# A spatial weight tile of a gated MLP scaled in quarters, three of them in earlier groups, with its row scales made in two parts

## The chip, the cores and the metric

The kernel runs on one core of a Trainium2 chip. The time is that of the device for one execution, in microseconds (us), and the median of several runs is given. The engines of the core are named as in the profile: PE (TensorE, matrix products), DVE (VectorE), ACT (ScalarE), POOL (GpSimd) and SP (SyncE, which here only issues transfers). Each engine works through its own list of instructions in order, and waits where an instruction needs what another engine or a transfer has not yet delivered.

## What is computed

The reference is a transformer block: attention in a dilated sliding window, then a gated MLP with a spatial weight. The change lies in the second half, of which this is the core (S = 2048 positions, D = 1024, F = 3584, Fh = 1792, bfloat16):

```python
def _B_ref(x, w_in, w_sp, b_sp, w_out):
    z = _gelu(jnp.einsum('bsd,df->bsf', x, w_in))
    z1 = z[..., :Fh].copy()
    z2 = _layernorm(z[..., Fh:], axis=-1)
    g = jnp.einsum('ts,bsf->btf', w_sp, z2) + b_sp[None, :, None]
    return jnp.einsum('bsf,fd->bsd', z1 * g, w_out)
h = x + _A_ref(_layernorm(x, axis=-1), A_wqkv, A_wo)
h2 = h + _B_ref(_layernorm(h, axis=-1), B_w_in, B_w_sp, B_b_sp, B_w_out)
```

`w_sp` is 2048 x 2048: a product over positions, not over features.

## The kernel before

The last part of the kernel, from line 1449 on, computes `g`, `z1 * g` and the product with `w_out`. It works in two halves (`pr` = 0 and 1), each for 1024 output positions. A half has seven **groups** (`i`, numbered through as `n` = 0 to 13), each of 256 features, and then four **tile pairs** (`q`, numbered through as `w` = 0 to 7), each of 256 positions times `w_out`.

Both products are done with seven block products in place of eight (Strassen's way with Winograd's sums). So PE's operands are partly blocks and partly sums of blocks, which DVE makes beforehand: `z_form` (line 1209) for a group, `s_form` (line 1447) for a tile pair, `t_forms` (lines 1185 to 1191) for the spatial weight of a half, and `wform` (line 1430) for `w_out`. A block product in a group is eight matmuls on PE (line 1274, in `times`); the results come out of PSUM by ACT copies (lines 1484, 1489, 1338), DVE additions (lines 1542, 1558, 1570, 1578) and POOL additions (lines 1505, 1545, 1546, 1565). In a tile pair POOL adds `p5` to `p7` (line 1660) and `u` to `p7` (line 1688), and DVE ends with a multiply-add of `p7` into the residual row `h2` (line 1709); then the rows are stored.

**The spatial weight** comes as four tiles `raw[0]` to `raw[3]` of 512 output positions each, 128 partitions x 16 x 512, transposed by the load (`load_raw`, line 1173). Tiles 0 and 1 belong to the first half, 2 and 3 to the second; `rawa` is the name of tiles 0 and 2 in the profile, `rawb` that of 1 and 3. In fp16 its products would leave the range of the type, so every row of `w_sp` is scaled by a power of two (`scale_raw`, line 1178, half a tile at a time, 128 x 4096, in place, bfloat16 to fp16) and the result is scaled back at the end (`rv`). How the scales come about: ACT sums the absolute values of each 128 rows (`row_sum`, line 1128), DVE makes the powers of two (`row_scales`, seven small instructions, lines 1132 to 1138), PE turns them from a column to a row (line 1498), ACT copies the row out of PSUM and stores it to DRAM (lines 1500, 1501), and SP loads it, spread over all partitions, into `rows` (`rows_in`, line 1158).

For the second half, the sums of the eight row blocks 8 to 15 are made in groups 1 to 4, two blocks in each. The scales of all eight are made in group 5, after the third product of the group, together with the level of `w_out` (`wout_level`, lines 1393 to 1398, which line 1499 turns on PE). Tile 2 comes in four loads of 128 positions in groups 2 to 5, and is scaled by halves: the first at the end of group 6, the second in tile pair 1. Tile 3 is loaded in tile pair 0 and scaled in tile pair 2, by halves as well, one ahead of and one behind line 1709. The sums of tiles 2 and 3 (`t_forms(1, ...)`) follow in tile pair 3, and PE's first products of group 7 are mixed in there.

Orders: the program's text gives the order on PE, DVE, ACT, POOL and, from the start of this part, SP (`manual_schedule`). Buffers are shared by rotation: two for `p7`, five for the forms, six banks of PSUM. The scheduler of the first part (class `Order`) is touched only in that two helpers take other arguments, with the same instructions as before.

Of the kernel before, what the change touches and what calls it, by code (L numbers as in the profile page):

```python
# [12 lines left out]
FP16 = mybir.dt.float16  # L13
I32 = mybir.dt.int32
ALU = mybir.AluOpType
# [7 lines left out]
P = 128  # L23
NT = S // P
CH = 512
NCH = S // CH
TPC = CH // P
TPP = 2 * TPC
# [18 lines left out]
HK = S // P // 2  # L47
# [21 lines left out]
class Order:  # L69
# [6 lines left out]
    def add(self, eng, us, fn, deps=(), prio=5.0, lat=0.1, take=None, free=None, table=None):  # L76
        o = _Op()
        o.eng, o.us, o.fn, o.prio, o.lat, o.free, o.table = eng, us, fn, prio, lat, free, table
        o.take = (take,) if isinstance(take, str) else take or ()
        o.deps = [d if isinstance(d, tuple) else (d, d.lat) for d in deps if d is not None]  # L80
        o.start, o.end, o.n = None, None, len(self.ops)
        self.ops.append(o)
        return o
# [49 lines left out]
def kernel(  # L133
# [13 lines left out]
    V, A, T = nc.vector, nc.scalar, nc.tensor  # L147
    dma = nc.sync.dma_start
# [14 lines left out]
    rs_d = dpool.tile([NT, P], BF16, name="rs_d")  # L163
# [3 lines left out]
    ident = cpool.tile([P, P], BF16, name="ident")  # L167
# [12 lines left out]
    rsc16 = cpool.tile([P, NT], BF16, name="rsc16")  # L180
    rscT = cpool.tile([P, P], BF16, name="rscT")
# [220 lines left out]
    add = o_.add  # L402
    G = {}
# [694 lines left out]
    raw, frm, wt_ = {}, {}, {}  # L1098
    wabs_ops = []
# [27 lines left out]
        h_ = wn[i][:, hf * D:(hf + 1) * D]  # L1127
        A.activation(h_, h_, ACTF.Abs, accum_out=wabs[:, i, hf:hf + 1])

    def row_scales(pr):  # L1130
        n = slice(pr * TPP, (pr + 1) * TPP)
        V.tensor_tensor(wlim[:, n], wabs[:, n, 0], wabs[:, n, 1], op=ALU.add)
        V.tensor_tensor(wlim[:, n], wlim[:, n], babs[:, n], op=ALU.add)
        V.tensor_scalar(wlim[:, n], wlim[:, n], 2.0 ** -40, 2.0 ** 60, op0=ALU.max, op1=ALU.min)
        V.tensor_scalar(wexp[:, n], wlim[:, n].bitcast(I32), 0x7F800000, None, op0=ALU.bitwise_and)
        V.tensor_scalar(rsc[:, n], wexp[:, n], -1.0, float(261 << 23), op0=ALU.mult, op1=ALU.add)
        V.tensor_scalar(rinv[:, n], wexp[:, n], float(-(7 << 23)), None, op0=ALU.add)
        V.tensor_copy(rsc16[:, n], rsc[:, n].bitcast(FP32))
# [13 lines left out]
        A.copy(rscT[0:TPP, :], wt_["ps"][0:TPP, 0, 0:P])  # L1152
        dma(rs_d[0:TPP, :], rscT[0:TPP, :])

    def rows_in(pr):
        if pr == 0:
            wt_["rows"] = zpools["z"].tile([P, S], BF16, name="rows")
        dma(wt_["rows"][:, 2 * pr * CH:(2 * pr + 2) * CH],
            rs_d[pr * TPP:(pr + 1) * TPP, :].rearrange("i p -> (i p)").unsqueeze(0).to_broadcast([P, 2 * CH]))

    def bias_in(pr):
        cols = slice(2 * pr * CH, (2 * pr + 2) * CH)
        wt_["b", pr] = wt_["rows"][:, 0:2 * CH] if pr else bp.tile([P, 2 * CH], BF16, name="brow", tag="xr", bufs=XRB)[:]
        dma(wt_["b", pr], B_b_sp[cols].unsqueeze(0).to_broadcast([P, 2 * CH]))

    def bias_rows(pr):
        cols = slice(2 * pr * CH, (2 * pr + 2) * CH)
        V.tensor_tensor(wt_["rows"][:, cols], wt_["rows"][:, cols], wt_["b", pr], op=ALU.mult)
# [6 lines left out]
    def scale_raw(c, k0, n=HK):  # L1175
        ks = slice(k0, k0 + n)
        rows = wt_["rows"][:, c * CH:(c + 1) * CH].unsqueeze(1).to_broadcast([P, n, CH])
        V.tensor_tensor(raw[c][:, ks, :].bitcast(FP16), raw[c][:, ks, :], rows, op=ALU.mult)  # L1178

    def t_forms(pr, n):  # L1180
        a, b = raw[2 * pr][:].bitcast(FP16), raw[2 * pr + 1][:].bitcast(FP16)
        if n < 3:
            frm[pr, n] = zpools["z"].tile([P, HK, CH], FP16, name=f"form{n}")
        if n == 0:
            V.tensor_tensor(frm[pr, 0][:], b[:, 0:HK, :], a[:, 0:HK, :], op=ALU.subtract)
        elif n == 1:
            V.tensor_tensor(frm[pr, 1][:], b[:, HK:NT, :], frm[pr, 0][:], op=ALU.subtract)
        elif n == 2:
            V.tensor_tensor(frm[pr, 2][:], a[:, HK:NT, :], frm[pr, 1][:], op=ALU.subtract)  # L1189
        else:  # L1190
            V.tensor_tensor(b[:, 0:HK, :], b[:, HK:NT, :], b[:, 0:HK, :], op=ALU.subtract)
# [46 lines left out]
    bs_ = add("ACT", 0.3, bias_size, [bt_], prio=2.0, free="acc")  # L1238
    level1 = w1_level()
# [17 lines left out]
        zpools["ps"] = ctx.enter_context(tc.tile_pool(name="psA", bufs=2, space=PSUM, side="right"))  # L1257

    def rows_first():
        rows_in(0)  # L1260
        bias_in(0)

    head(NCH - 1)
    rs_ = add("DVE", 1.0, lambda: row_scales(0), [G["avdone", NCH - 1], bs_, level1] + wabs_ops, prio=2.8)
    rt_ = add("PE", 0.1, rows_turned, [rs_], prio=0.5, take="acc", lat=0.2)
    ro_ = add("ACT", 0.3, rows_out, [rt_], prio=1.0, free="acc")
    rl_ = dma_op(4.0, rows_first, [(ro_, 2.5), G["close"]])
# [4 lines left out]
    def times(dst, wts, mov, first, lo=0, hi=HK, last=HK):  # L1272
        for k in range(lo, hi):
            T.matmul(dst, wts(k), mov(k), start=(first and k == 0), stop=(k == last - 1), skip_group_check=not first)  # L1274

    def slab(t):
        return lambda k: t[:, k, :]
# [45 lines left out]
    def bank(dt=FP32):  # L1323
        return psB.tile([P, CH if dt == FP32 else 2 * CH], dt, name="bank", tag="bank", bufs=6)
# [35 lines left out]
    kb = p2.tile([P, 8], BF16, name="kb", tag="kb", bufs=1)  # L1360
# [30 lines left out]
    def wout_level():  # L1391
        l2 = l1n.rearrange("p (f j) -> p f j", j=2)
        V.tensor_tensor(kf, l2[:, :, 0], l2[:, :, 1], op=ALU.max)
        V.tensor_tensor(kf, kf, rf, op=ALU.mult)
        V.tensor_reduce(kk[:, 0:1], kf, axis=AX.X, op=ALU.max)
        V.tensor_scalar(kk[:, 0:1], kk[:, 0:1], 2.0 ** -60, 2.0 ** 90, op0=ALU.max, op1=ALU.min)
        V.tensor_scalar(kk[:, 0:1].bitcast(I32), kk[:, 0:1].bitcast(I32), 0x7F800000, None, op0=ALU.bitwise_and)
        V.tensor_copy(kb[:, 0:1], kk[:, 0:1])
# [50 lines left out]
    for pr in range(NCH // 2):  # L1449
# [5 lines left out]
        for i in range(NQ):  # L1455
            n = pr * NQ + i
# [34 lines left out]
                seven()  # L1491
                times(k3[:], slab(zs[n, 4]), slab(b22), False)
            times(k2[:], slab(zs[n, 2]), slab(t2_), True)
            if pr == 0 and i == 5:
                row_scales(1)
                wout_level()
                turned = bank(BF16)
                T.transpose(turned[0:TPP, 0:P], rsc16[:, TPP:NT], ident[:])
                T.transpose(turned[0:1, P:2 * P], kb[:, 0:1], ident[:])
                A.copy(rscT[0:TPP, :], turned[0:TPP, 0:P])  # L1500
                A.dma_start(rs_d[TPP:NT, :], rscT[0:TPP, :])
            if n not in (0, 1, NQ, NQ + 1):
                row_two(n, b21)
            times(k4[:], slab(a22), slab(t4_), False)
# [14 lines left out]
            if more:  # L1519
                if n in (0, NQ):  # L1520
                    if n == 0:
                        z_form(n + 1, 3)
                    z_form(n + 1, 1)
                if n == NQ:
                    bias_rows(1)
                if n == 0:
                    V.memset(ones[:], 1.0)
                    feature_scales()
            elif pr == 1:
                for m in (3, 1, 2, 4):  # L1530
                    s_form(TPC, m, 0, NQ - 1)
            else:
                for fp in range(4, NQ):
                    wout_scaled(fp)
                scale_raw(2, 0)
            if n + 2 < 2 * NQ:
                load_z2f(n + 2, 1)
            if n == 5:
                rows_in(1)
            if n == 0:  # L1540
                z1_scaled(n)
            V.tensor_tensor(u[:], k2[:], p1[:], op=ALU.add)
# [48 lines left out]
        for q in range(TPC):  # L1591
# [109 lines left out]
                nc.gpsimd.tensor_tensor(p7[:], p7[:], u[:], op=ALU.add)  # L1701
            if pr:
                V.scalar_tensor_tensor(h1[:, 0:CH], k1[:], r1, h1[:, 0:CH], op0=ALU.mult, op1=ALU.add)
            if pr == 0 and q < 3:
                (lambda: None, lambda: scale_raw(2, HK), lambda: scale_raw(3, 0))[q]()
            if pr:
                V.scalar_tensor_tensor(h2[:, 0:CH], k4[:], r2, (u if end else p5)[:], op0=ALU.mult, op1=ALU.add)
            if not end:
                V.scalar_tensor_tensor(h2[:, CH:D], p7[:], r2, h2[:, CH:D], op0=ALU.mult, op1=ALU.add)  # L1709
            if end:  # L1710
                dma(out2d[t1_ * P:(t1_ + 1) * P, 0:CH], h1[:, 0:CH])
                dma(out2d[t2_ * P:(t2_ + 1) * P, :], h2[:])
                for n, (lo, hi) in enumerate(((0, cut), (cut, CH))):
                    V.scalar_tensor_tensor(h1[:, CH + lo:CH + hi], k3[:, lo:hi], r1, p1[:, lo:hi], op0=ALU.mult, op1=ALU.add)
                    (dma if n else A.dma_start)(out2d[t1_ * P:(t1_ + 1) * P, CH + lo:CH + hi], h1[:, CH + lo:CH + hi])
            else:
                if pr:
                    V.scalar_tensor_tensor(h1[:, CH:D], k3[:], r1, p1[:], op0=ALU.mult, op1=ALU.add)
                for t, hr in ((t2_, h2), (t1_, h1)):
                    dma(out2d[t * P:(t + 1) * P, :], hr[:])  # L1720
# [34 lines left out]
```

## Time and profile before

| | |
|---|---|
| median of 3 runs | 689.41 us (689.26 to 689.83) |
| the profiled execution | 689.43 us, span 687.6 us |
| PE busy | 679.7 us, 99% |
| DVE busy | 591.8 us, 86% |
| ACT, POOL busy | 357.5 us, 168.3 us |
| granted TensorE clock | 1.00 |

The span runs from the first to the last instruction. Group 0 begins at about 433 us, and a group takes some 12 us; the tile pairs of the first half lie from 512 to 554, group 7 starts in the course of pair 3, and the last pair ends at 684. A row of a timeline gives the start, the length, the engine, the line, the operation, the tiles (out<-in), the shape, and in brackets the idle time of the engine ahead of it with what ended it. Matmuls overlap: eight matmuls in a row take 1.9 us from start to end, but the next eight start 1.73 us after them.

### The profile page before, as it was taken

The numbers are of one execution on the slowest core, as the hardware profiler recorded it, in microseconds if no ns is written. First come the engines' busy times: TensorE is split into PE (matmuls) and PEld (weight loads), VectorE is DVE, ScalarE is ACT, GpSimd is POOL, SyncE is SP. The second block draws the span as 40 slices with busy tenths as digits, with TensorE's granted clock in tenths as the row PEclk, the third lists the DMA queues.
The fourth block names the chain that finished last, engine by engine and source line by source line (L and its number), as shares of the span: only waits on it lengthen the run. The fifth ranks groups of instructions, "written<-read, shape, count | busy, mean of one in ns | idle before, by whom it ended". The sixth has DMA issues, their size and how long they took to land.

```text
span 687.6 us, 9194 instructions
## 1 busy us (share of the span) xinstructions
PE 679.7 (99%) x3423; PEld 360.1 (52%) x3440; DVE 591.8 (86%) x750; ACT 357.5 (52%) x529; POOL 168.3 (24%) x147
## 2 busy tenths in 40 slices
PE   9999999999999999999999999999999999999997
PEld 6766666566645445444544467444444443444443
DVE  6899899998999989998897878997889999755565
ACT  4547652354229998774882556387671131324121
POOL 0100010010210101000120134474541316553442
PEclk9999999999999999999999999999999999999999
DMA  9979588667995469444483996999967214642031
GB/s 314 335 245 247 172 194 273 154 164 270 217 346 222 98 247 231 168 173 107 122 226 120 206 269 200 302 291 325 244 209 184 98 59 124 186 121 94 1 113 71
DMA packets 143933, 133.07 MB, mean 194 GB/s; under 512 B 68752, under 2 KB 115504, under 8 KB 143760
## 3 DMA queue, kind: packets, MB, share of 16 engines
q1 hardware_dynamic: 132720, 88.93, 45.3%
q0 software_dynamic: 8416, 34.80, 18.2%
q10 hardware_dynamic: 2752, 8.75, 3.8%
q8 instruction: 27, 0.44, 0.3%
q14 instruction: 18, 0.15, 0.1%
HBM read 75.25 MB, written 33.10 MB: 158 GB/s over the span
## 4 chain that ended last, share of the span: by engine, by line
PE 92%; DVE 7%; issue 1%; POOL 0%; DVEq 0%; ACT 0%
PE acc L468 22%; PE bank L1274 22%; PE acc L800 14%; PE acc L868 11%; PE banka L1274 8%; PE acc L723 8%; PE acc L1040 2%; PE acc L310 2%; DVE zs L1209 1%; PE wps L232 1%; DVE rawb L1178 1%; DVE hr L1709 1%; DVE bank L1692 1%; PE acc L1004 1%; DVE hr L1693 0%
## 5 line engine op out<-in xcount | busy, mean ns | idle before, releaser
L800 PE MATMUL acc<-win,hnT 128*128 128x512 bf16 (+1 forms) x501 | 97.4, 352 | 0.6
L800 PEld LDWEIGHTS <-hnT 128*128 128x128 bf16 x512 | 49.9, 98 | 47.5 <-issue 0.7
L532 DVE TENSOR_TENSOR prod<-qT,kT 128x4096 bf16<-128x4096 bf16 x32 | 72.7, 2283 | 1.6 <-ACT kT L474 1.3
L868 PE MATMUL acc<-hnT,win 128*128 128x512 bf16 x336 | 73.7, 379 | 0.0
L1274 PEld LDWEIGHTS <-zs 128*128 128x128 f16 x448 | 43.3, 98 | 54.9 <-DVE zs L1209 3.7
L479 ACT CAST stg<-acc 128x1024 bf16<-128x1024 f32 x36 | 36.4, 1012 | 61.2 <-PE acc L468 54.7
L468 PE MATMUL acc<-xnT,wk 128*128 128x512 bf16 x256 | 56.5, 379 | 0.0
L468 PE MATMUL acc<-xnT,wv 128*128 128x512 bf16 x256 | 56.4, 380 | 0.0
L723 PE MATMUL acc<-wo_sb,av_oT 128*128 128x512 bf16 x250 | 55.8, 379 | 0.3
L1274 PEld LDWEIGHTS <-z 128*128 128x128 bf16 x336 | 32.7, 98 | 40.3 <-DVE form L1189 1.2
L868 PEld LDWEIGHTS <-win 128*128 128x128 bf16 x336 | 32.7, 98 | 39.5 <-issue 0.7
L1274 PE MATMUL bank<-rawb,zs 128*128 128x512 f16 x224 | 52.8, 379 | 0.4 <-DVE zs L1209 0.4
L1274 PE MATMUL banka<-rawa,z 128*128 128x512 f16 x224 | 52.0, 379 | 0.0
L1274 PE MATMUL bank<-form,zs 128*128 128x512 f16 x224 | 50.9, 379 | 0.8 <-DVE zs L1209 0.8
L468 PEld LDWEIGHTS <-wk 128*128 128x128 bf16 x256 | 36.5, 143 | 19.0 <-issue 0.8
L468 PEld LDWEIGHTS <-wv 128*128 128x128 bf16 x256 | 36.5, 144 | 18.6 <-issue 0.5
L468 PE MATMUL acc<-xnT,wq 128*128 128x512 bf16 x192 | 41.9, 379 | 0.0
L723 PEld LDWEIGHTS <-av_oT 128*128 128x128 bf16 x256 | 24.9, 98 | 29.8
L807 ACT ACTIVATE u<-acc 128x1024 bf16<-128x1024 f32 (+1 forms) x32 | 29.2, 911 | 19.9 <-PE acc L800 19.7
L536 DVE TENSOR_TENSOR prod<-prod 128x2048 bf16<-128x2048 bf16 x32 | 38.7, 1216 | 0.0
L1274 PEld LDWEIGHTS <-sf 128*128 128x128 f16 x231 | 22.4, 98 | 26.3
L468 PEld LDWEIGHTS <-wq 128*128 128x128 bf16 x192 | 27.5, 143 | 13.9
(325 smaller groups left out, 1237.5 us busy)
## 6 DMA issues: line engine op xcount, KB each, us to landing
z<-z_d SPq DMA_DIRECT2D x28, 512.0 KB, 5.3
qkv_d<-stg SPq DMA_DIRECT2D x36, 256.0 KB, 4.6
wn<-in_B_w_sp_dram ACTq DMA_DIRECT2D x16, 512.0 KB, 4.8
z1c<-z_d SPq DMA_DIRECT2D x14, 512.0 KB, 4.8
z_d<-z1s SPq DMA_DIRECT2D x21, 256.0 KB, 2.6
z_d<-u SPq DMA_DIRECT2D x12, 448.0 KB, 2.6
av_y<-av_z POOLq DMA_DIRECT2D x4, 1024.0 KB, 9.8
av_oT<-av_zz POOLq DMA_DIRECT2D x4, 1024.0 KB, 15.1
```

What stands on the lines that cost most here:

```text
L232: T.matmul(wps[:], warm[:, 0:P], warm[:], start=True, stop=True)
L310: T.matmul(dst.rearrange("p (a b) -> p a b", b=P), wqs[:, kt, dl, :], xnT[0][:, lo:hi, kt, :], start=start, stop=stop)
L468: T.matmul(G[key][:, j, :].rearrange("p (a b) -> p a b", a=TPC), wv[:, kt, dl, :], xnT[c][:, :, kt, :], start=(kt == 0), stop=(kt == KT - 1))
L479: A.copy(stg[:], G[key][:])
L532: V.tensor_tensor(st["prod"][:], qT[:], kT[:, :, o:o + CH], op=ALU.mult)
L536: V.tensor_tensor(dst, p_[:, 0:4, :], p_[:, 4:8, :], op=ALU.add)
L723: T.matmul(st["acc", il][:, nh, :], oTs[c][:, dl, il * P:(il + 1) * P], wo_sb[:, dl, nh * CH:(nh + 1) * CH], start=(dl == 0), stop=(dl == ...
L800: T.matmul(accf[:, n0:n1], hnTs[c][:, il, kt, :], wins[hf][:, kt, n0:n1], start=(kt == 0), stop=(kt == KT - 1))
L807: A.activation(st["u", il][:, hf * 1024:hf * 1024 + wd], G["accz", c, il, hf][:].rearrange("p a b -> p (a b)")[:, 0:wd], ACTF.Gelu_apprx_t ...
L868: T.matmul(G["accy", c, fp][:, j, :].rearrange("p (a b) -> p a b", a=TPC), wt[:, kt, f0 * P:(f0 + 1) * P], hnTs[c][:, :, kt, :], start=(kt ...
L1040: T.matmul(d_, wt, mv, start=(not again and j == 0 and kt == 0), stop=(j == len(fps) - 1 and kt == 3), skip_group_check=bool(again))
L1274: T.matmul(dst, wts(k), mov(k), start=(first and k == 0), stop=(k == last - 1), skip_group_check=not first)
```

## The change

- `row_scales` and `rows_in` take a range of row blocks. The scales of blocks 8 to 11 are made, turned, stored and loaded in group 3, those of 12 to 15 in group 5. So the seven DVE instructions, the transposition on PE, ACT's copy and store and SP's load are there twice, each for four blocks.
- A new helper `scale_tile` scales a quarter of a tile: 128 of its 512 positions, through all 16 blocks (128 x 16 x 128). Tile 2 is scaled by it: quarters 0 and 1 in group 4, quarter 2 in group 5 ahead of the row scales, quarter 3 at the end of group 6 where its first half was scaled.
- The scaling of tile 2's second half in tile pair 1 is gone.
- In tile pair 2, line 1709 comes ahead of the scaling of tile 3's first half.

```diff
-    def row_scales(pr):
-        n = slice(pr * TPP, (pr + 1) * TPP)
+    def row_scales(lo, hi):
+        n = slice(lo, hi)
...
-        dma(wt_["rows"][:, 2 * pr * CH:(2 * pr + 2) * CH],
-            rs_d[pr * TPP:(pr + 1) * TPP, :].rearrange("i p -> (i p)").unsqueeze(0).to_broadcast([P, 2 * CH]))
+        dma(wt_["rows"][:, lo * P:hi * P],
+            rs_d[lo:hi, :].rearrange("i p -> (i p)").unsqueeze(0).to_broadcast([P, (hi - lo) * P]))
...
+    def scale_tile(c, il):
+        cols = slice(il * P, (il + 1) * P)
+        rows = wt_["rows"][:, c * CH + il * P:c * CH + (il + 1) * P].unsqueeze(1).to_broadcast([P, NT, P])
+        V.tensor_tensor(raw[c][:, :, cols].bitcast(FP16), raw[c][:, :, cols], rows, op=ALU.mult)
...
             times(k2[:], slab(zs[n, 2]), slab(t2_), True)
-            if pr == 0 and i == 5:
-                row_scales(1)
-                wout_level()
+            if pr == 0 and i == 4:
+                scale_tile(2, 0)
+                scale_tile(2, 1)
+            if pr == 0 and i in (3, 5):
+                t0 = TPP if i == 3 else TPP + TPC
+                if i == 5:
+                    scale_tile(2, 2)
+                row_scales(t0, t0 + TPC)
+                if i == 5:
+                    wout_level()
                 turned = bank(BF16)
-                T.transpose(turned[0:TPP, 0:P], rsc16[:, TPP:NT], ident[:])
-                T.transpose(turned[0:1, P:2 * P], kb[:, 0:1], ident[:])
-                A.copy(rscT[0:TPP, :], turned[0:TPP, 0:P])
-                A.dma_start(rs_d[TPP:NT, :], rscT[0:TPP, :])
+                T.transpose(turned[0:TPC, 0:P], rsc16[:, t0:t0 + TPC], ident[:])
+                if i == 5:
+                    T.transpose(turned[0:1, P:2 * P], kb[:, 0:1], ident[:])
+                A.copy(rscT[0:TPC, :], turned[0:TPC, 0:P])
+                A.dma_start(rs_d[t0:t0 + TPC, :], rscT[0:TPC, :])
...
-                scale_raw(2, 0)
+                scale_tile(2, 3)
...
-            if n == 5:
-                rows_in(1)
+            if n in (3, 5):
+                rows_in(TPP if n == 3 else TPP + TPC, TPP + TPC if n == 3 else NT)
...
-            if pr == 0 and q < 3:
-                (lambda: None, lambda: scale_raw(2, HK), lambda: scale_raw(3, 0))[q]()
             if pr:
                 V.scalar_tensor_tensor(h2[:, 0:CH], k4[:], r2, (u if end else p5)[:], op0=ALU.mult, op1=ALU.add)
             if not end:
                 V.scalar_tensor_tensor(h2[:, CH:D], p7[:], r2, h2[:, CH:D], op0=ALU.mult, op1=ALU.add)
+            if pr == 0 and q == 2:
+                scale_raw(3, 0)
```

More of the change, by code (lines that the diff above doesn't have):

```diff
@@ L1153, in rows_out, with rows_in @@
         dma(rs_d[0:TPP, :], rscT[0:TPP, :])
-    def rows_in(pr):
-        if pr == 0:
+    def rows_in(lo, hi):
+        if lo == 0:
             wt_["rows"] = zpools["z"].tile([P, S], BF16, name="rows")
-        dma(wt_["rows"][:, 2 * pr * CH:(2 * pr + 2) * CH],
-            rs_d[pr * TPP:(pr + 1) * TPP, :].rearrange("i p -> (i p)").unsqueeze(0).to_broadcast([P, 2 * CH]))
+        dma(wt_["rows"][:, lo * P:hi * P],
+            rs_d[lo:hi, :].rearrange("i p -> (i p)").unsqueeze(0).to_broadcast([P, (hi - lo) * P]))
     def bias_in(pr):
@@ L1259, in rows_first @@
     def rows_first():
-        rows_in(0)
+        rows_in(0, TPP)
         bias_in(0)
     head(NCH - 1)
-    rs_ = add("DVE", 1.0, lambda: row_scales(0), [G["avdone", NCH - 1], bs_, level1] + wabs_ops, prio=2.8)
+    rs_ = add("DVE", 1.0, lambda: row_scales(0, TPP), [G["avdone", NCH - 1], bs_, level1] + wabs_ops, prio=2.8)
     rt_ = add("PE", 0.1, rows_turned, [rs_], prio=0.5, take="acc", lat=0.2)
```

## The prediction

> **What bounds the kernel now.** I read the busy table first, then the chain of work that ended last, then the timelines of the engines in the last 250 us.
>
> ```profile
> PE 679.7 (99%) x3423; PEld 360.1 (52%) x3440; DVE 591.8 (86%) x750; ACT 357.5 (52%) x529; POOL 168.3 (24%) x147
> PE 92%; DVE 7%; issue 1%; POOL 0%; DVEq 0%; ACT 0%
> ```
>
> PE is busy 99% of the span, so an edit that moves vector work can only win what PE idles, and can lose as much as it makes PE wait. The chain names the one place where DVE sets the end (start, length, engine, tile, line):
>
> ```profile
> 538.37 2.20 DVE rawa L1178
> 540.57 1.67 DVE hr L1709
> ...
> 548.73 2.28 DVE rawb L1178
> 551.01 1.67 DVE hr L1709
> 552.68 2.20 DVE rawb L1178
> ```
>
> It runs on DVE from 533.15 to 582.65 without a break. The third spatial tile's second half (538.37) is in it, and so is the multiply-add of line 1709, 1.67 long here. PE in the same place (start, length, what, idle time before and its releaser):
>
> ```profile
> 567.06 1.90 PE L1274 MATMUL bank<-form,z 128*128 128x512 f16 x8 [0.71 <-DVE form L1189]
> ...
> 570.84 1.90 PE L1274 MATMUL bank<-rawb,zs 128*128 128x512 f16 x8 [0.16 <-DVE zs L1209]
> 573.50 3.70 PE L1274 MATMUL bank<-form,zs 128*128 128x512 f16 x16 [0.76 <-DVE zs L1209]
> ```
>
> A fourth wait, 0.27, stands at 582.65. What they cost in all: a block of eight matmuls takes 1.727 us (group 8 to 9, 584.38 to 596.47, is 12.09 for seven). From 554.10, the first block of the second half, to 641.36 there are 49 blocks, 84.62 us; they took 87.26. **PE loses 2.64 us there, and that is the most that the change can win.**
>
> **What is taken from that place.** The second half's scaling leaves: 2.28 by its row, 2.20 from its start to the next instruction. It would seem that line 1709 shrinks too, since it takes 0.74 at 530.18 and 1.75 behind each scaling, which would make 2.20 + 2 x 1.01 = 4.2 us. POOL's rows speak against that:
>
> ```profile
> 505.75 2.65 POOL L1505 TENSOR_TENSOR p<-p,p 128x512 f32<-128x512 f32 x1 [6.24 <-ACT p L1489]
> 548.97 3.16 POOL L1660 TENSOR_TENSOR p<-p,p 128x512 f32<-128x512 f32 x1 [2.19 <-ACT p L1651]
> ```
>
> The same additions take 1.26 to 1.27 alone. The one at 548.97 begins while DVE scales (548.73 to 551.01) and ends at 552.13, some 1.15 after that scaling; line 1709 begins at 550.92 and ends 0.54 after POOL. So the two take turns, and the 1.01 is POOL's turn, which will fall on another DVE instruction. The Trainium skill (SBUF — State Buffer, "Who interferes with whom") has this as a rule: a DVE instruction with two SBUF inputs and a GpSimd instruction that reads SBUF share a port, and the later one blocks wholly. By the rule the gain is the 2.1 below; by the plain subtraction it would be 4.2, cut to 2.64 by PE's idle time; this trace agrees with the rule.
>
> With turns the chain is, walked by the starts in the rows: line 1709 of pair 1 at 538.29 (POOL idle, 0.67 to the next start), forms of pair 3 at 538.96 and 539.50; POOL's addition, ready at 539.91, takes its 1.2 at 540.05; the other two forms 541.25 to 542.40 (the PE product that frees the last one's buffer ends at 540.7, so it isn't late). Line 1680 then starts at 542.40 where it was 544.69. The six instructions to line 1709 keep their spacing: 1709 of pair 2 at 546.44, now first; tile 3's first half 547.11 to 549.31; POOL (ready 548.9) 1.2; second half 550.50 to 552.70; line 1665; the first form tile at 553.38 instead of 555.47. **DVE arrives 2.09 earlier, and the swap by itself wins nothing**: it moves POOL's turn from line 1709 to the second scaling. Later instructions wait on DVE or on POOL behind it and shift alike, so PE keeps 2.64 - 2.09 = 0.55 of its loss. Bounds: 2.64 if POOL's turns fall into gaps, and 2.09 - 1.2 = 0.9 if one more falls on the chain.
>
> **What is added earlier.** Four quarters of 128x2048. No row has this shape with runs of 128; a quarter tile as 128x2048 in runs of 512 takes 1.21 to 1.22 (line 1178 in the first half, 1.14 from start to start), and the forms of line 1209 read runs of 128 at 0.68 for 1024, the same rate. I take 1.14; the upper bound is the 2.28 of a whole half.
>
> Two quarters come in group 4, ahead of line 1542:
>
> ```profile
> 478.96 0.68 DVE L1584 TENSOR_TENSOR zg<-zg,z1c 128x1024 f16<-128x1024 f16 x1
> 482.19 0.69 DVE L1542 TENSOR_TENSOR u<-bank,p 128x512 f32<-128x512 f32 x1 [2.55 <-PE bank L1274]
> ...
> 483.85 0.69 DVE L1558 TENSOR_TENSOR zg<-banka,rows 128x512 f16<-128x512 f32 x1 [0.37 <-PE banka L1274]
> ...
> 485.64 0.69 DVE L1570 TENSOR_TENSOR zg<-bank,p 128x512 f16<-128x512 f32 x1 [0.51 <-PE bank L1274]
> ```
>
> DVE waits 2.55 there for PE, and 2.28 fits. POOL's addition, ready at 481.0, waits to 481.9 and holds the next form to 483.1; the gaps of 0.37 and 0.51 take that up. Cost 0, with 3.43 - 2.28 = 1.15 to spare.
>
> Group 3 gets row scales for four tiles: seven small DVE instructions, 1.17 (490.97 to 492.14 in group 5), in DVE's 1.58 idle ahead of line 1542 (468.52 to 470.10); the sums they need were finished by ACT at 461.8. The result is there at 469.7, PE reaches its new transposition at 469.83. In group 5 the two transpositions take PE from 494.00 to 494.31, so one costs 0.1 to 0.3: **0.16**. ACT copies the result (0.25) and issues its store (0.53); waiting for PE it starts the row sums behind that some 2.1 later. Its gaps until line 1489 in group 4 are 0.66, 1.20 and 1.09, together 2.95: hidden; without them POOL's addition and the end of group 4 would come 2.1 later. The loads of the last two weight rows, issued by ACT, move from 473.08 to 475.2, and at 4.9 to landing arrive before their sums at 480.87.
>
> The row of scales must be in SBUF by 479.6. The store goes out at 470.4 to 470.9. The small store of group 5 was issued at 494.69 and read from 498.43, so it took at most 3.7; 256 KB stores land in a median of 2.0. The load stands on SP behind the one at 473.48, so it leaves at 473.9 to 474.2 and, at the 4.0 to 4.5 of its sisters (twice its size), lands by 478.7. Behind it on SP waits the load that left at 477.90 anyway, and then the third quarter's transposing load (478.31). Cost 0.
>
> Group 5: the third quarter comes ahead of the row scales and the output weight's level, whose last instruction (line 1398) ended at 493.17. It now ends at 494.31. Queued behind it on PE are the second transposition, at 494.15 before, and with the 0.06 that PE lags a DVE end it starts at 494.37: **0.22** lost on PE; bounds 0, and 1.2 if group 4 passes on 1 us. Line 1542 behind it on DVE waited for PE until 494.28 and is held no more than that. In group 6 one quarter replaces a half, 1.1 less, ending in a wait for PE: 0.
>
> **Sum.** The profiled execution took 689.43 (span 687.6), as good as the median of 689.41. 689.43 - 2.09 + 0.16 + 0.22 = **687.7**.
>
> **Rivals.** (a) *The whole idle time goes.* POOL's additions fall into gaps, and PE never waits: 689.43 - 2.64 + 0.1 to 0.3 = 687.0. For it: POOL is busy only 8.3 of the 21 us from 533 to 554; against: its addition of pair 3 is released by ACT at 548.9, inside a scaling either way. (b) *The wait is replaced.* One more turn of POOL on the chain (0.9 won), or group 4 passes 0.8 on to group 5's transposition: 689.43 - 0.9 + 0.4 or 689.43 - 2.09 + 0.16 + 1.0, 688.5 to 688.9. For it: DVE is 7.8 of 8 busy from 512 to 520 and POOL moves with its inputs. (c) *Slower: the row of scales is late.* DVE is in order, so a quarter in group 4 that waits for its row holds line 1542 and the forms behind it. From 479.6 the first 1.15 is covered; each us beyond holds the transposition in group 5, and PE, by one. It eats the gain of 1.7 at a landing at 482.5, and the kernel is slower by more than 0.2% from 483.9; at 485, 690.2. For it: the DMA engines were fully busy from 465 to 489. Against: 13 us for a store and a load that by the rows need 8.2 at most. (d) *The change doesn't do what it says*, a quarter waiting for a later load into the same tile. In the built program each quarter waits for its own load, so I give it no chance of its own.
>
> **Chances.** Forecast 0.62 (687.3 to 688.4), (a) 0.15, (b) 0.15, (c) 0.08. 0.2%, about what a measurement can tell from no change, is 1.38 us: faster is below 688.03. Three quarters of the forecast and all of (a) lie below it: 0.62. The rest of the forecast and (b), 0.30, are the same; (c) slower, 0.08. The range leaves out (c) and edges of the others: 686.9 (full 2.64, 0.1 paid) to 689.0.
>
> **What would show it.** Right: no L1178 on rawa between 533 and 554; the first form tile of the second half 2.1 earlier against PE; PE's waits at that place 0.3 to 0.7 in all; a POOL addition still near 2.4 long beside tile 3's scaling; about 0.2 more ahead of the second transposition in group 5, DVE without idle ahead of line 1542 in group 4. Wrong: idle of DVE ahead of the first quarter (rows late), PE waits in groups 4 to 6, quarters longer than 1.3, or PE idle near 2.6 after 560 as before.

## The result: the changed kernel is slower, and the profile after

| | before | after |
|---|---|---|
| median | 689.34 us (4 runs, 689.08 to 689.83) | 696.86 us (4 runs, 694.31 to 697.17) |
| ratio | | 1.010 [1.0076, 1.0125] |
| the profiled execution | 689.43, span 687.6 | 694.31, span 692.5 |

The change costs 7.5 us by the medians. The profile of the changed kernel is of its fastest execution, which is 4.9 us longer than that of before; the ledger below is that of these two. Lines have moved: 1274 is 1279, 1209 is 1214, 1542 is 1555, 1498 and 1499 are 1510 and 1512, 1709 is 1720; quarters run on line 1183.

The busy table and the chain of work that ended last, of the changed kernel:

```profile
PE 681.9 (98%) x3441; PEld 360.8 (52%) x3441; DVE 594.4 (86%) x759; ACT 357.8 (52%) x530; POOL 164.8 (24%) x147
PE 81%; DVE 13%; issue 3%; DMA 2%; POOL 1%; ACT 0%; DVEq 0%; SPq 0%; POOLq 0%
```

The chain has DMA in it, 2% of the span, which it had not before. PE's share of busy time falls from 99% to 98%.

Where it goes, by PE's starts at the same instructions of both profiles:

| stretch (from, to) | before | after | difference |
|---|---|---|---|
| group 0 to group 3 behind its new transposition | 433.54 to 469.83 | 433.21 to 470.54 | +1.04 |
| group 3 to the first block of the second half | 469.83 to 554.10 | 470.54 to 560.93 | +6.12 |
| the 49 blocks of the second half's groups | 554.10 to 641.36 | 560.93 to 645.93 | -2.26 |
| to the last wide block of the last pair | 641.36 to 682.34 | 645.93 to 686.91 | 0 |

Group 0's point comes 0.33 earlier in the second profile, and what lies behind the last block is 0.33 longer, so the differences add up to the 4.9 of the spans.

The third row is the gain that was forecast (2.09). The timeline there, of the changed kernel (start, length, engine, line, idle before):

```profile
553.22 0.74 DVE L1720 SCALAR_TENSOR_TENSOR hr<-p,rinv_w,hr 128x512 bf16<-128x512 f32 x1
553.88 5.56 DVE L1178 TENSOR_TENSOR rawb<-rawb,rows 128x4096 f16<-128x4096 bf16 x2
...
587.21 1.90 PE L1279 MATMUL bank<-rawb,zs 128*128 128x512 f16 x8 [0.22 <-DVE zs L1214]
```

Line 1720 takes 0.74 where its forerunner, line 1709, took 1.75 behind a scaling, and the two scalings behind it take 5.56 together, 1.2 over the two 2.2 of before: POOL's turn has moved from the one to the other. Of PE's waits only the 0.22 at 587.21 is left.

The loss is in groups 3 to 5. Queues and engines there:

```profile
473.73 0.77 POOL L1387 DMA_DIRECT2D wout_b<-in_B_w_out_dram  x1
474.66 0.55 SPq L1158 DMA_DIRECT2D rows<-rs_d  x1
484.81 2.36 DVE L1183 TENSOR_TENSOR rawa<-rawa,rows 128x2048 f16<-128x2048 bf16 x2 [5.45 <-DMA rows<-rs_d]
...
498.23 0.22 PE L1510 MATMUL bank<-ident,rsc 128*4 128x128 bf16 x1 [3.09 <-DVE rsc L1138]
499.31 0.22 PE L1512 MATMUL bank<-ident,kb 128*1 128x128 bf16 x1 [0.86 <-DVE kb L1403]
499.45 3.42 PE L1279 MATMUL banka<-rawa,z 128*128 128x512 f16 x8
```

SP issued the load of the row of scales at 474.66, and the quarters of group 4 could start at 484.81: 10.15 us behind the issue, where the prediction had 4.0 to 4.5. DVE stood idle for 5.45, everything behind it on DVE was late, and PE waited 3.09 and 0.86 at group 5's transpositions. About 1 us of that has a second cause: one of the seven small instructions ahead of the first transposition, 0.16 in group 3, lost a turn to POOL:

```profile
496.08 1.26 POOL L1518 TENSOR_TENSOR p<-p,p 128x512 f32<-128x512 f32 x1 [3.45 <-ACT p L1494]
496.23 1.13 DVE L1133 TENSOR_TENSOR wlim<-wlim,rstd 128x4 f32<-128x4 f32 x1
```

And the eight products behind these waits take 3.42 instead of the 1.90 of before:

```profile
494.31 1.90 PE L1274 MATMUL banka<-rawa,z 128*128 128x512 f16 x8
```

The changed kernel's windows say why (start:end, PE busy, PEld, DVE, ACT, POOL, each with its instructions, then granted PE clock, DMA share, GB/s):

```profile
497.00:499.00 2.00, 0.22 (x1) 0.08 (x1) 1.76 (x11) 0.00 (x0) 0.34 (x1) 1.00 1.28 227
499.00:500.00 1.00, 0.69 (x3) 0.34 (x4) 0.94 (x4) 0.26 (x1) 0.10 (x1) 0.84 0.75 279
500.00:501.00 1.00, 1.00 (x4) 0.35 (x3) 0.86 (x7) 0.00 (x0) 1.00 (x1) 0.50 0.57 216
501.00:502.00 1.00, 1.00 (x4) 0.41 (x3) 0.66 (x2) 0.00 (x0) 0.92 (x2) 0.50 0.00 0
502.00:503.00 1.00, 1.00 (x4) 0.30 (x2) 0.09 (x1) 0.00 (x0) 0.92 (x2) 0.50 0.00 0
503.00:504.00 1.00, 1.00 (x6) 0.44 (x5) 1.00 (x2) 0.00 (x0) 1.00 (x1) 0.96 0.00 0
```

PE, nearly idle for 4 us, got half its clock for some 3.4 us. Its three blocks from 499.45 to 506.54 take 7.09 where they took 5.40 before (494.31 to 499.71): 1.69 more.

Group 3 lost its 1.04 in another way. Of the changed kernel:

```profile
468.50 0.17 DVE L1134 TENSOR_SCALAR wlim<-wlim 128x4 f32<-128x4 f32 x1
468.64 1.26 POOL L1518 TENSOR_TENSOR p<-p,p 128x512 f32<-128x512 f32 x1 [2.80 <-ACT p L1494]
468.70 1.23 DVE L1135 TENSOR_SCALAR wexp<-wlim 128x4 int32<-128x4 int32 x1
...
470.39 0.22 PE L1510 MATMUL bank<-ident,rsc 128*4 128x128 bf16 x1 [0.72 <-DVE rsc L1138]
```

The fourth of the seven small instructions, 0.17 elsewhere, takes 1.23: POOL's addition had begun 0.06 before it. So the result came 1.06 later, and PE waited 0.72.

### The profile page after: what moved, and what is told of

It reads as the page before. It is cut to its first block, busy times and chain, and to the rows that moved or that the text cites. A ratio compares the mean times of both kernels' runs of the same rounds, so it can differ in the third digit from the quotient of the medians.

```text
span 692.5 us, 9229 instructions
## 1 busy us (share of the span) xinstructions
PE 681.9 (98%) x3441; PEld 360.8 (52%) x3441; DVE 594.4 (86%) x759; ACT 357.8 (52%) x530; POOL 164.8 (24%) x147
## 4 chain that ended last, share of the span: by engine, by line
PE 81%; DVE 13%; issue 3%; DMA 2%; POOL 1%; ACT 0%; DVEq 0%; SPq 0%; POOLq 0%
PE acc L468 22%; PE bank L1279 15%; PE acc L800 14%; PE acc L868 11%; PE acc L723 8%; PE banka L1279 6%; DVE zs L1214 2%; PE acc L310 2%; PE acc L1040 2%; DMA rows<-rs_d 1%; DVE zg L1597 1%; DVE rawb L1178 1%; DVE rawb L1196 1%; DVE form L1190 1%; DVE form L1192 1%
## 5 line engine op out<-in xcount | busy, mean ns | idle before, releaser
L1279 PE MATMUL banka<-rawa,z 128*128 128x512 f16 x224 | 53.5, 387 | 0.0
L1128 ACT ACTIVATE wn<-wn 128x1024 bf16<-128x1024 bf16 x32 | 33.5, 1053 | 2.7 <-DMA wn<-in_B_w_sp_dram 2.1
```

## The experiments

The first theory (A): the loss is the late row of scales, with what follows from it. Its rivals: the quarters, or the added small instructions, cost the time wherever the row stands.

**1. A row that is there.** The changed kernel, with quarters 0 and 1 of group 4 scaled by the first half's part of `rows`, which has long been in SBUF (the new argument of `scale_tile` is the place in `rows`); the late load still runs. This kernel leaves out the two quarters' own scales.

```diff
-                scale_tile(2, 0)
-                scale_tile(2, 1)
+                scale_tile(2, 0, 0)
+                scale_tile(2, 1, P)
```

> The changed kernel, but quarters 0 and 1 of tile 2 are multiplied by row scales of the first half, which lie in SBUF long before (so the output is not the reference's); every instruction stays. Theory A (the late row of scales costs the time: DVE stands 5.45 us in group 4, and PE 3.95 us in group 5 behind it, after which PE's clock drops): no idle ahead of the quarters in group 4, PE's wait at the two transpositions of group 5 under 1 us, clock 1.00 there; 689.4 + 1.0 (transposition of group 3) + 0.3 (group 5) - 2.3 (pair boundary) = 688.4, between 687.7 and 689.0. Rival B (the added instructions and waits themselves cost it, whatever the load does): 694 to 697 as the changed kernel.

Measured: 688.76 us (10 runs, 688.46 to 688.98), ratio 0.999 [0.9981, 1.0000]. Its timeline:

```profile
470.62 0.22 PE L1511 MATMUL bank<-ident,rsc 128*4 128x128 bf16 x1 [0.73 <-DVE rsc L1138]
...
479.50 2.35 DVE L1184 TENSOR_TENSOR rawa<-rawa,rows 128x2048 f16<-128x2048 bf16 x2
```

The two quarters follow without idle time, and PE waits for nothing in groups 4 and 5; the granted clock is 1.00 throughout 498 to 504, and the second half's groups take 84.99 (555.29 to 640.28). 8.1 us of the median hang on the wait for the row and what follows from it. Theory A is shown. Group 3's 0.73 is still there, as it must be.

**2. Group 3's wait.** The same, with group 3's transposition, copy and store two products later on PE, behind the fifth product and ACT's row sums.

```diff
-                turned = bank(BF16)
-                T.transpose(turned[0:TPC, 0:P], rsc16[:, t0:t0 + TPC], ident[:])
...
+                def turn(t0=t0):
+                    t = bank(BF16)
+                    T.transpose(t[0:TPC, 0:P], rsc16[:, t0:t0 + TPC], ident[:])
...
                 if i == 5:
...
+                    turned = turn()
...
+                if i == 3:
+                    turn()
                 for f in WSUM.get(i, ()):
```

> The run with rows already there (quarters 0 and 1 scaled by the first half's row scales, which lie in SBUF, so the output is not the reference's), with group 3's transposition, its copy and its store moved behind the fifth product and the row sums. Theory (PE waited 0.73 in group 3 because one of the seven small DVE instructions lost a turn to POOL, and nothing else was behind that loss): PE has no wait at that transposition, 0.6 to 0.8 faster than 688.76, so 688.0 to 688.2. Rival (the transposition costs PE about 1 us wherever it stands, by the switch to another shape and back): 688.6 to 688.9.

Measured: 687.98 (10 runs, 687.65 to 688.27), ratio 0.9978 [0.9968, 0.9988]. PE meets the transposition at 473.54 without a wait, and no wait is left in groups 3 to 5. From group 0 to the second half it takes 121.06 where experiment 1 took 121.86. So 0.8 of group 3's loss is the wait behind POOL's turn (line 1135 still takes 1.23, but PE no longer stands behind it). (The row's load now leaves at 480.85: a kernel that needs this row in group 4 can't have it so.)

**3. Why the row is late.** Theory A1: it is the burst in which the load stands, 1 MB of `w_out` issued by POOL 0.93 ahead of it above all. Rival B1: store and load take that long one behind the other, whatever else moves. Two kernels move the `w_out` load, one ahead to group 2, one back into group 4:

```diff
-            if n == 3:
+            if n == 2:
                 load_wout(4)
```

> The changed kernel with the 1 MB load of w_out that POOL issues in group 3 (at 473.7) issued in group 2. Theory A1 (the row's load lands late because it shares the DMA engines with a burst of some 2.6 MB that starts at the same moment): 1 MB less at some 350 GB/s lets it land about 3 us earlier, DVE's idle ahead of the quarters falls from 5.45 to 2 to 3 us, PE waits 1 to 2 us in group 5 in place of 3.95, and the clock drop shrinks; 690 to 692.5. Rival B1 (the load is slow by its own form, 128 copies of one short row, or by its place behind another load on SP): lands 10 us after its issue as before, 694 to 697.

Measured: 692.57 (4 runs, 691.59 to 693.51), ratio 1.0047 [1.0032, 1.0062]. The `w_out` load left at 464.44, but then a transposing load held SP 7.05 us, so the row's load left 1.9 later, at 476.57; the quarters began at 483.19, 6.6 behind the issue, DVE idle 3.33. Better, not cured, and a little over the 690 to 692.5 that was expected. With no `w_out` load within 12 us the row still took 6.6: the two 512 KB loads of line 1124 left at 476.56, the row's own moment, but whether it is they that held it, no run shows.

```diff
+                if i == 4:
+                    load_wout(4)
                 for f in WSUM.get(i, ()):
...
-            if n == 3:
-                load_wout(4)
```

> The changed kernel with the 1 MB load of w_out that POOL issues in group 3 (at 473.7) issued in group 4 (about 482), after the row's load should have landed. Theory A1 (burst): the row's load lands 6 to 8 us after its issue in place of 10.1, without the delay of its issue that the earlier load brought; DVE's idle ahead of the quarters 2 to 3 in place of 5.45; 690 to 692.5. Rival B1 (its own form or place): 10 us as before, 694 to 697.

Measured: 690.80 (7 runs, 689.97 to 693.14), ratio 1.0033 [1.0017, 1.0049]. Its timeline:

```profile
474.80 0.52 SPq L1158 DMA_DIRECT2D rows<-rs_d  x1
479.16 2.35 DVE L1183 TENSOR_TENSOR rawa<-rawa,rows 128x2048 f16<-128x2048 bf16 x2
483.13 0.77 POOL L1387 DMA_DIRECT2D wout_b<-in_B_w_out_dram  x1
...
490.66 1.06 ACT L1382 ACTIVATE zg<-wout_b 128x1024 f16<-128x1024 bf16 x1 [4.18 <-DMA wout_b<-in_B_w_out_dram]
...
496.61 0.22 PE L1512 MATMUL bank<-ident,kb 128*1 128x128 bf16 x1 [1.44 <-issue]
```

The same load, issued at the same place (474.80), was there by 479.16, at most 4.36 later, where 6 to 8 were expected: that the `w_out` load ahead of it makes the row late is shown, and B1 falls. What is left over 688.8 is a new lateness: the `w_out` load now lands so late that ACT waits 4.18 for it, the level of `w_out` comes late, and PE waits 1.44 for its transposition.

**4. Quarters behind the work.** The changed kernel, with quarters 0 and 1 behind group 4's last multiplication on DVE, where nothing of group 4 stands behind them.

```diff
-            if pr == 0 and i == 4:
-                scale_tile(2, 0)
-                scale_tile(2, 1)
...
             V.tensor_tensor(zg[:, 2 * i + 1, :], zg[:, 2 * i + 1, :], z1c[:, 1, :], op=ALU.mult)
+            if pr == 0 and i == 4:
+                scale_tile(2, 0)
+                scale_tile(2, 1)
```

> The changed kernel with quarters 0 and 1 moved to the end of group 4, behind its last multiplication on DVE (before quarter 2 and the row scales of group 5). Theory A (what hurts is that line 1555 and the forms stand behind a quarter that waits for its row): the row is there by then, DVE has no idle ahead of the quarters, but three quarters in a row (3.4 us) put the level of w_out 2.5 us behind PE, so PE waits 2 to 3 us in group 5; 690.0 to 692.5, the upper part if the clock drops again. Rival B: 694 to 697.

Measured: 693.07 (4 runs, 690.91 to 693.72), ratio 1.0049 [1.0031, 1.0066]; the median lies above the expected 692.5, the profiled execution (690.91) within. The row landed 9.8 after its issue, and nothing waited for it. But now three quarters stand in one row on DVE (491.89 to 495.37) ahead of the row scales, and PE waits 1.43 and 0.86 at the transpositions of group 5. The place of a late row's user is not enough; what stands ahead of group 5's small instructions counts too.

**5. The swap by itself.** The kernel before, with only its line 1709 ahead of tile 3's first scaling.

```diff
-                (lambda: None, lambda: scale_raw(2, HK), lambda: scale_raw(3, 0))[q]()
+                (lambda: None, lambda: scale_raw(2, HK), lambda: None)[q]()
...
                 V.scalar_tensor_tensor(h2[:, CH:D], p7[:], r2, h2[:, CH:D], op0=ALU.mult, op1=ALU.add)
+            if pr == 0 and q == 2:
+                scale_raw(3, 0)
```

> The kernel before with only the order changed in tile pair 2: line 1709 ahead of the scaling of tile 3's first half. Theory (POOL and DVE take turns; POOL's turn moves from line 1709 to the second scaling): line 1709 takes 0.74 in place of 1.75, one of the two scalings 3.3 to 3.5 in place of 2.28, the time within 0.3 us of the kernel before. Rival (the turn vanishes): 1.0 us faster, 688.4.

Measured: 689.45 (10 runs, 689.15 to 689.86), ratio 1.0001 [0.9991, 1.0011]; the second half's groups take 87.33 (554.17 to 641.50), as before. Its timeline:

```profile
548.79 0.74 DVE L1709 SCALAR_TENSOR_TENSOR hr<-p,rinv_w,hr 128x512 bf16<-128x512 f32 x1
549.45 5.56 DVE L1178 TENSOR_TENSOR rawb<-rawb,rows 128x4096 f16<-128x4096 bf16 x2
```

Line 1709 is 1.01 shorter and the scalings 1.2 longer together: the swap only moves POOL's turn, as predicted.

**6. The pair boundary's gain without early rows.** The kernel before, its row of scales as it was, with tile 2's second half taken out of tile pair 1: once in two pieces into DVE's gaps of group 6 (ahead of lines 1558 and 1578), once whole at the end of group 6.

```diff
+            if n == NQ - 1:
+                scale_raw(2, HK, 4)
             V.tensor_tensor(z11, k1[:], bt1, op=ALU.add)
...
+            if n == NQ - 1:
+                scale_raw(2, HK + 4, 4)
             V.tensor_tensor(z12, k3[:], u[:], op=ALU.add)
```

> The kernel before, with tile 2's second half scaled in two pieces of 128 x 2048 in group 6, ahead of the two additions for which DVE idles 0.68 and 1.03 us there (lines 1558 and 1578), and no longer in tile pair 1. No row scales are made earlier. Theory (the gain at the pair boundary, 2.26 in the changed kernel, is that of DVE's 2.2 us alone and needs nothing of the early row scales): from the first block of the second half to tile pair 4 85.0 to 85.5 us in place of 87.26, and 687.2 to 688.0. Rival (DVE has no room in group 6 either, as it is busy 97% from 512 to 533: the 2.2 us arrive at the boundary as before, or PE waits in tile pair 0): 689.0 to 690.

Measured: 688.83 (10 runs, 688.39 to 688.99), ratio 0.9990 [0.9980, 1.0000].

```diff
                 scale_raw(2, 0)
+                scale_raw(2, HK)
             if n + 2 < 2 * NQ:
```

> The kernel before, with tile 2's second half scaled right behind its first half at the end of group 6. Line 1542 of group 6 then starts 2.6 us later or, with a turn of POOL between the halves, 3.4; the gaps of 0.68 and 1.03 and those of 0.23 and 0.43 in tile pairs 0 and 1 take up most of it. Theory: half to all of the boundary's gain is left, 687.5 to 688.8, less than with the two pieces in the gaps. Rival: PE waits in tile pair 0 for the late forms, 689 to 691.

Measured: 689.27 (10 runs, 688.97 to 689.47), ratio 0.9998 [0.9988, 1.0007]. Both are slower than expected (687.2 to 688.0, 687.5 to 688.8), the second as its rival had it. In both the second half's groups take 85.76, a gain of 1.5, and both give back a part of it in the first tile pair, where PE waits for a product of group 6. The first and the second kernel's timelines:

```profile
515.41 0.60 PE L1274 MATMUL banka<-wout_b,zg 128*128 128x512 f16 x2 [0.59 <-DVE zg L1585]
```

```profile
515.76 0.60 PE L1274 MATMUL banka<-wout_b,zg 128*128 128x512 f16 x2 [1.18 <-DVE zg L1582]
```

At neither of these places does group 6 take the whole half without a wait of PE; to use groups 4 and 5 for it takes an early row.

**7. All of it in time.** The changed kernel with three pieces moved: the `w_out` load to the start of group 4, the row scales ahead of the last multiplication of groups 2 and 4 (so ahead of POOL's addition), the third quarter behind the level. And the same without the first piece.

```diff
+            if n == 4:
+                load_wout(4)
             if pr == 0 and 2 <= i < 2 + TPC:
...
                 if i == 5:
-                    scale_tile(2, 2)
-                row_scales(t0, t0 + TPC)
-                if i == 5:
                     wout_level()
+                    scale_tile(2, 2)
...
-            if n == 3:
-                load_wout(4)
...
+            if pr == 0 and i in (2, 4):
+                row_scales(*((TPP, TPP + TPC) if i == 2 else (TPP + TPC, NT)))
             V.tensor_tensor(zg[:, 2 * i + 1, :], zg[:, 2 * i + 1, :], z1c[:, 1, :], op=ALU.mult)
```

> The change with three pieces moved: the four tiles of w_out loaded at the start of group 4 in place of the middle of group 3 (about 476 us, behind the row of scales on the queues), each row_scales one DVE instruction earlier (ahead of the last product with z1c of group 2 and of group 4, so ahead of POOL's addition of group 3), and in group 5 the third quarter behind wout_level. Theory (the row of scales lands late only in the burst; the rest of the loss is the two transpositions' waits and the clock after them): the row lands by 480, DVE waits under 0.5 us ahead of the first quarters, PE waits under 0.3 us at each transposition, no slow products at 499 to 503, and the time is the 694.31 of the profiled execution less 6.1 (group 5) and 0.9 (group 3): 687.3, between 686.9 and 688.2. Rival (any load beside the tile's own transposing loads is late, or the w_out load now comes late for its sums): DVE or ACT waits over 2 us in group 4, and 689 or more.

Measured: 688.16 (11 runs, 687.63 to 688.48), ratio 0.9980 [0.9971, 0.9988]: faster than both kernels with the whole computation in it. Its timeline:

```profile
475.18 0.33 SPq L1158 DMA_DIRECT2D rows<-rs_d  x1
475.58 0.91 POOL L1387 DMA_DIRECT2D wout_b<-in_B_w_out_dram  x1
482.46 2.65 DVE L1183 TENSOR_TENSOR rawa<-rawa,rows 128x2048 f16<-128x2048 bf16 x2 [3.27 <-DMA rows<-rs_d]
...
495.14 0.22 PE L1512 MATMUL bank<-ident,kb 128*1 128x128 bf16 x1 [0.26 <-issue]
```

The time is the theory's, though the row is not: it took 7.28 where a landing by 480 was expected, and DVE idled 3.27. That lateness no longer reaches PE, which waits 0.26 and keeps its full clock; experiment 3's first kernel, with DVE idle for 3.33 and the small instructions behind the third quarter, waited 1.49 and 0.86. From group 0 to the second half it pays 0.68 (433.84 to 555.08 is 121.24, before it was 120.56) and gains 2.25 in the 49 blocks (555.08 to 640.09): 1.57 won. Of that the profiled execution (688.48) keeps 0.95: its group 0 starts 0.30 later, and 0.32 goes behind the blocks.

> The same without the first piece: the w_out load stays in group 3, the row of scales in its burst. Theory: the row lands 9 to 10 us after its issue, at about 484, and DVE waits some 5 us there as in the changed kernel; the seven small instructions of group 3 leave PE no wait there (0.7 less), and in group 5 wout_level and row_scales no longer stand behind a quarter of 1.2 us, so that PE's two waits fall from 3.95 us to 1 to 2.5 us: 690.0 to 692.5. Rival (the row's lateness is not what costs; the small instructions' place is): as fast as the kernel with all three pieces, under 688.5.

Measured: 693.92 (5 runs, 693.16 to 695.56), ratio 1.0073 [1.0059, 1.0087], outside the theory's 690.0 to 692.5, on the far side from the rival. Its timeline:

```profile
473.58 0.77 POOL L1387 DMA_DIRECT2D wout_b<-in_B_w_out_dram  x1
474.19 0.52 SPq L1158 DMA_DIRECT2D rows<-rs_d  x1
486.35 2.36 DVE L1183 TENSOR_TENSOR rawa<-rawa,rows 128x2048 f16<-128x2048 bf16 x2 [7.13 <-DMA rows<-rs_d]
...
498.12 0.22 PE L1508 MATMUL bank<-ident,rsc 128*4 128x128 bf16 x1 [1.46 <-DVE rsc L1138]
499.80 0.22 PE L1510 MATMUL bank<-ident,kb 128*1 128x128 bf16 x1 [1.46 <-DVE kb L1403]
```

The row took 12.16 in the burst, 2 more than in the changed kernel, and forms of group 4 came late as well (PE waits of 0.73 and 1.18 there). The one difference to the kernel ahead of it is 1 MB issued 2.0 us earlier: 5.8 us of the median.

**The row's landing** (us, by the profile's rows of the transfers, so a little less than to a first quarter that waits):

| kernel | `w_out` load issued | row's load issued | landed after |
|---|---|---|---|
| `w_out` in group 4's middle (3) | 483.13 | 474.80 | 4.1 |
| `w_out` in group 2 (3) | 464.44 | 476.57 | 6.5 |
| all in time (7) | 475.58 | 475.18 | 7.2 |
| quarters at the end of group 4 (4) | 473.92 | 474.86 | 9.8 |
| the changed kernel | 473.73 | 474.66 | 10.1 |
| a row that is there (1) | 473.95 | 474.89 | 11.2 |
| without the first piece (7) | 473.58 | 474.19 | 12.1 |

For experiment 2's row, for which no quarter waits, the profile has no landing. The three kernels with the `w_out` load 0.93 or 0.94 ahead differ among themselves by 1.4. To issue it 0.40 behind the row does not make the row quick either (7.2).

## Why the prediction was wrong

Forecast 687.7, range 686.9 to 689.0, against 696.86 (694.31 in the profiled execution). Rival (c) came true, at 0.08.

- **The pair boundary: right.** 2.09 predicted, 2.26 measured; line 1709 shrinks, the second scaling grows by POOL's turn, the swap wins nothing (experiment 5). The rule that the prediction drew on, of the Trainium skill (SBUF — State Buffer, "Who interferes with whom"), agrees with the 5.56 of the two scalings.
- **"lands by 478.7. Cost 0": wrong, and the step that failed.** The landing was priced at 4.0 to 4.5 by its sisters, ahead of which no load of `w_out` had just been issued. It took 10.2 behind 1 MB issued 0.93 earlier, and 4.4 at most with that load gone. The contrary evidence was on the table ("the DMA engines were fully busy from 465 to 489") and was weighed against durations that had not been measured under that load.
- **The consequence: right in kind.** The row needed by 479.6, with 1.15 of cover, came at 484.8: 4.05 beyond, and PE's two waits in group 5 are 3.95. That the two agree is partly luck. Counted from each profile's group 0, the third quarter came 3.2 later than in experiment 1 (494.91 against 491.92, with group 0 at 433.21 and 433.43). The other 0.97 is the turn of POOL at line 1133 (1.13 instead of 0.16), which no term had. By the prediction's rate a landing at 485 gives 687.7 + 4.25, about 692, so the 690.2 given for (c) was an error of arithmetic.
- **Not foreseen: the clock.** 1.69 us for three blocks at half clock behind the waits. Of group 5's stretch, 6.12 in all, 3.95 are waits and 1.69 clock; the rest, 0.48, holds the transpositions, foreseen at 0.22.
- **"0.16" in group 3: 1.04.** Seven instructions of 1.17 in 1.58 of idle left 0.14 to PE. POOL starts its addition in that same gap. The prediction had used turns at the boundary and forgot them here; the wait is removed by a later transposition (experiment 2) or by earlier small instructions (7).
- **The quarters themselves: right.** 1.14 to 1.2 each, free in group 4 where their row is there (experiment 1).
- **Smaller readings.** The loads of the last two weight rows, priced at 4.9 to landing, took a median of 8.4, and ACT waited 2.11 for them ahead of 483.81; in experiment 1 it waited 1.28, and PE lost nothing by it. And the chain from 533.15 to 582.65 is not DVE's "without a break": an addition of POOL (line 1545) holds 1.54 us of it, from 574.72.

The sum with the measured terms: 687.7, plus 0.88 (group 3), plus 5.90 (groups 4 and 5), less 0.17 (boundary), is 694.31, the profiled execution. The other three executions, 696.68 to 697.17 at mean clocks of 0.994 to 0.996, have no trace here; where their further 2.4 to 2.9 us went stays open.

## What to carry to other kernels

Price a transfer by what it takes beside the load that is in flight at its place, not by its sisters' median; where the DMA engines are full, ask which large transfer is issued within a few microseconds of it and whether it can move: 0.4 us behind was still too near here, 8 us was far enough. A small operand that DVE needs in order is worth such a distance, and its user a place with no small, urgent work behind it. When a late transfer makes PE idle for some microseconds, reckon with slow products behind the idle time as well.

## What was not expected of the hardware

**Half a clock after split waits.** In experiment 3 with the earlier `w_out` load PE waited only 1.49 and 0.86, with a transposition in between, and still lost its clock:

```profile
497.14 0.22 PE L1510 MATMUL bank<-ident,rsc 128*4 128x128 bf16 x1 [1.49 <-DVE rsc L1138]
498.22 0.22 PE L1512 MATMUL bank<-ident,kb 128*1 128x128 bf16 x1 [0.86 <-DVE kb L1403]
498.37 3.57 PE L1279 MATMUL banka<-rawa,z 128*128 128x512 f16 x8
```

Nearly the same waits, 1.43 and 0.86, in experiment 4's profile, and 1.46 and 1.46 in the last kernel's, left the clock at 1.00. The Trainium skill (TensorE: Matmul & The Clock Gate, "HAM oscillation — how this bites in real kernels") gives the rule that PE should have no idle gap over some 3.4 us; the drop after 1.49 and 0.86 speaks against reading it as a limit for one gap. The Trainium skill (the same page, "What's actually happening") says that activity is watched in free-running windows of about 3.4 us; the slow stretch of the changed kernel, from about 499.7 to 503.1, has that length. Whether the windows' phase decides which kernel is hit, no run here shows.

The mean clock of all executions points the same way. In the five kernels whose profiles show 1.4 us or more of PE waits in group 5, 15 of 24 executions have a mean clock of 0.998 or less, and in the four that have both they take 0.8 to 3.2 us more than the fastest at 0.999 or 1.00; in the other six, all 61 executions have 0.999 or 1.00.

**A tiny instruction can lose a whole turn.** 128 x 4 elements, 0.17 us elsewhere, took 1.23 in group 3 beside POOL's addition of 1.26, and 1.13 in group 5.
